# Three heads per softmax transpose and value matmul, spread by masked copies, in a two-layer recurrent-memory attention kernel

## The chip, the cores and the metric

The kernel runs on one core of one Trainium2 chip. The metric is device time in microseconds (us), from the first to the last instruction of one launch; the figure given for a kernel is the median of its runs. The engines are named as the profile names them: PE (TensorE matmuls), PEld (TensorE weight loads), DVE (VectorE), ACT (ScalarE), POOL (GpSimd) and SP (the queue from which most transfers are issued).

## What is computed

The reference runs two identical layers over 2048 tokens of width 512. A layer is attention with a recurrent memory (A), followed by a gated feed-forward part (B), each behind a layernorm and a residual. Cut to what matters:

```python
# A: 64 segments of 32 tokens; 8 memory rows go from one segment to the next
for s in range(64):
    h = concatenate([mem, x[s*32:(s+1)*32]])        # 40 rows of 512
    q, k, v = h @ Wq, h @ Wk, h @ Wv                # 32 heads of 128
    scores = where(mask, (q @ k.T) * 128**-0.5, -1e9)   # 40 x 40 per head
    o = softmax(scores) @ v                         # 40 x 128 per head
    o = sum over heads and features of o * Wo       # 40 x 512
    mem = o[:8];  out[s] = o[8:]
# B: (sigmoid(x @ w_gate) * (x @ w_up)) @ w_down, hidden width 1792
x = x + A(layernorm(x)); x = x + B(layernorm(x))    # twice
```

The memory makes a layer's attention a chain of 64 segments: segment s+1 can't form its queries before segment s has been multiplied by Wo.

## The kernel before

**Steps.** Both layers run at once, the second one six segments behind the first (`LAG`), so there are 70 steps (`emit_step`). In 58 of them two segments, one of each layer ("jobs"), share every instruction: their 2 x 40 = 80 columns stand side by side in the tile `hT` (512 features on 128 partitions x 4 chunks). In the first six and last six steps there is one job with 40 columns.

**One step** works through the 32 heads in six groups: five of six heads and one of two. A group is three "units", and a unit is a pair of heads (k, 16+k). For each group:

- Q and K (L730): per head 2 x 4 matmuls of 128x128 weights against 80 columns; one ACT copy per three heads takes them into `qku` (L1024; three such tiles).
- scores (L744): one matmul per head. The weights are the head's Q from `qku`, read as 80 columns; the moving operand is its K.
- softmax on DVE and ACT: mask added per job (L758), maximum, subtraction, exponential (L768), sum, reciprocal, product (L775) into `pb`, in which every head has 64 columns, 40 of them used.
- transpose (L787): one matmul per unit turns two heads of `pb` (80 rows x 128 columns) into 128 rows x 80 columns. The keys of the first head of the pair land on partitions 0 to 39, those of the second on 64 to 103.
- spread: two copies per group, on ACT (L1024) or DVE (L1026), take these two partition ranges into `ptsb`. Each head has its own column range there, and the rest of `ptsb` was zeroed once at the start, so that the tile is block-diagonal: in a head's columns only that head's rows are not zero.
- values (L808): one matmul per unit and job. The weights are 104 rows of `vsb` (the values of both heads, at the same partitions), the moving operand is 2 heads x 40 columns of `ptsb`.
- output (L826): after an ACT copy into `otsb`, 4 matmuls per head accumulate the product with Wo in one bank `WB`, from which DVE writes the next step's memory columns (L839).

**Values.** Most rows of V don't depend on the memory. They are computed in blocks ahead of time (`v_pass`, L584), written to DRAM (`scr`) and fetched per step (L685). The 16 rows of each job that touch the memory are computed in the step itself (`add_strips`, L698): 32 matmuls of 512 columns, two copies into the single tile `sst`, then eight transfers from `sst` to `vsb` (L710). `vsb` is three tiles of 1024 columns; a step uses two of them, one for heads 0 to 7 and 16 to 23, one for the others.

**The rest** is work of the feed-forward part (`ffn`: L926 gate and up, L950 down) and of `v_pass`; it fills PE between the steps' own work.

**Order.** Instructions are not issued in program order. `Planner` gets every piece of work as a task with an engine, a duration, what it reads and writes and which buffers it needs, and makes one fixed order per engine from them (`forward` and `backward`, 24 rounds, the one with the shortest planned span is kept). Engines then run that order strictly, each waiting for the others by semaphores. Durations are formulas in the code, such as these:

```python
def mm_ns(n):
    return max(n / 2.4 + 2.3, 26.0)
def copy_ns(n, half=False):
    return {"ACT": n * 0.833 + 52.0, "DVE": n / (1.92 if half else 0.96) + 73.0}
```

A task that names two engines (the spread copies do) is put on either by the planner. Copies that read one PSUM bank are not put on two engines at once.

## Time and profile before

| | before |
|---|---|
| median of 3 runs | 1829.39 us (1826.49 to 1831.26) |
| the profiled run, its time and its span | 1827.17 us, 1825.3 us |
| granted TensorE clock | 0.998 of full |
| ACT busy, DVE busy | 1194.2 us (65%), 1162.9 us (64%) |
| POOL busy | 569.9 us (31%) |
| transfers | 272.11 MB, mean 149 GB/s |
| scores L744: matmuls, columns | 1856 of 80 and 384 of 40 |
| transposes L787 | 1120 of 80 |
| value matmuls L808 | 2048 of 80 |
| spread copies | 546 on ACT, 294 on DVE |

How it is read: "busy" is the time in which at least one instruction of an engine was under way. The matmuls of one engine overlap: one takes about 200 ns from start to end, but the next one starts long before that. What a matmul costs is the time from its start to the start of the next one, and this is read from the timeline of a short window, where the profile merges like instructions into one row: start, time from first start to last end, engine, line, operation, tiles, shapes, and how many.

### The profile page before, as it was taken

To read this page: it belongs to the slowest core of one execution; us is meant where nothing else is said; L and a number is where in the kernel's file an instruction comes from. 1 tells how busy PE (TensorE), PEld (TensorE's weight loads), DVE (VectorE), ACT (ScalarE), POOL (GpSimd) and SP (SyncE) were. 2 spreads that over 40 slices of the span, in tenths; PEclk is the share of its full clock that TensorE was granted. 3 is DMA by queue.
4 is the path that set the end of the run, shared out by engine and by line. 5 is a ranking of instruction groups with operands and counts; after the bars stand their busy time and mean duration, and the time that the engine had idled before them with its cause. 6 is when DMAs were issued, how large, how long until landed. Compare 5 with 4: busy or idle time off the path is not lost.

```text
span 1825.3 us, 92117 instructions
## 1 busy us (share of the span) xinstructions
PE 1776.6 (97%) x39783; PEld 1533.6 (84%) x39970; DVE 1162.9 (64%) x3927; ACT 1194.2 (65%) x3005; POOL 569.9 (31%) x817
## 2 busy tenths in 40 slices
PE   7999999999999999999999999999999999999998
PEld 4678788988898888988898898888888898888886
DVE  5466655676666666666666667656666676656665
ACT  5666666676666666666666666666666666676664
POOL 5223032413233242413324141323324241333422
PEclk9999999999999999999999999999999999999999
DMA  9734254535445364535446363545536353544543
GB/s 351 233 108 148 62 155 121 163 100 176 147 153 157 103 204 122 170 109 169 149 124 187 109 194 100 170 131 155 158 110 196 117 168 95 173 144 127 174 124 107
DMA packets 138441, 272.11 MB, mean 149 GB/s; under 512 B 32954, under 2 KB 70594, under 8 KB 138034
## 3 DMA queue, kind: packets, MB, share of 16 engines
q0 software_dynamic: 56640, 183.09, 32.1%
q1 hardware_dynamic: 81394, 83.12, 15.4%
q8 instruction: 313, 5.13, 1.2%
q14 instruction: 94, 0.77, 0.1%
HBM read 221.85 MB, written 27.26 MB: 136 GB/s over the span
## 4 chain that ended last, share of the span: by engine, by line
PE 81%; DVE 9%; ACT 4%; SPq 3%; issue 2%; DMA 1%; POOLq 0%; ACTq 0%; DVEq 0%
PE bank L730 28%; PE bank L826 16%; PE bank L926 10%; PE bank L698 7%; PE bank L584 6%; PE bank L950 4%; PE bank L744 4%; PE bank L808 3%; DVE st L758 3%; SPq L485 3%; PE bank L787 2%; ACT ptsb L1024 1%; DVE pb L775 1%; DVE mx L763 1%; ACT qku L1024 1%
## 5 line engine op out<-in xcount | busy, mean ns | idle before, releaser
L730 PE MATMUL bank<-hT,wq_sb 128*128 128x80 bf16 (+1 forms) x8960 | 621.6, 198 | 3.5 <-issue 1.3
L730 PE MATMUL bank<-hT,wk_sb 128*128 128x80 bf16 (+1 forms) x8960 | 620.5, 198 | 3.2 <-DMA wk_sb<-in_A_Wk_dram 3.2
L1024 ACT CAST qku<-bank 128x480 bf16<-128x480 f32 (+3 forms) x770 | 391.1, 513 | 233.5 <-PE bank L730 165.7
L730 PEld LDWEIGHTS <-wq_sb 128*128 128x128 bf16 x8960 | 455.8, 99 | 38.5 <-issue 23.9
L730 PEld LDWEIGHTS <-wk_sb 128*128 128x128 bf16 x8960 | 450.6, 99 | 4.4 <-DMA wk_sb<-in_A_Wk_dram 3.6
L758 DVE TENSOR_TENSOR st<-bank,maskb 80x240 f32<-80x240 f32 (+1 forms) x732 | 267.9, 367 | 245.5 <-PE bank L744 238.7
L826 PE MATMUL bank<-otsb,wo_sb 128*128 128x80 bf16 (+1 forms) x8960 | 370.2, 198 | 9.6 <-ACT otsb L1024 8.1
L826 PEld LDWEIGHTS <-wo_sb 128*128 128x128 bf16 x8960 | 345.4, 99 | 35.0 <-issue 11.3
L918 POOL DMA_DIRECT2D wg<-in_B_w_gate_dram x217 | 164.7, 759 | 573.7 <-PE bank L926 520.2
L1024 ACT CAST otsb<-bank 128x480 bf16<-128x480 f32 (+3 forms) x420 | 199.9, 485 | 66.0 <-PE bank L808 51.7
L944 POOL DMA_DIRECT2D wd<-in_B_w_down_dram x217 | 154.2, 712 | 231.0 <-PE bank L744 88.7
L1024 ACT COPY ptsb<-bank 40x240 bf16<-40x240 bf16 (+3 forms) x546 | 170.8, 315 | 53.0 <-PE bank L787 46.0
L768 ACT ACTIVATE st<-st 80x240 f32<-80x240 f32 (+3 forms) x420 | 160.6, 383 | 45.8 <-DVE st L765 42.6
L770 DVE TENSOR_REDUCE mx<-st 80x6 f32<-80x240 f32 (+3 forms) x420 | 151.6, 364 | 50.7 <-ACT st L768 47.2
L926 PE MATMUL bank<-xnT,wg 128*128 128x128 bf16 (+2 forms) x1784 | 171.8, 218 | 2.0 <-issue 1.5
L926 PE MATMUL bank<-xnT,wu 128*128 128x128 bf16 (+2 forms) x1784 | 171.1, 218 | 0.0
L919 POOL DMA_DIRECT2D wu<-in_B_w_up_dram x217 | 162.7, 750 | 1.2 <-PE bank L926 0.5
L744 PE MATMUL bank<-qku 128*80 128x80 bf16 (+1 forms) x2240 | 160.2, 204 | 2.2 <-ACT qku L1024 1.6
L775 DVE TENSOR_TENSOR pb<-st,mx 80x240 bf16<-80x240 f32 (+3 forms) x420 | 154.9, 369 | 4.0
L765 DVE TENSOR_TENSOR st<-st,mx 80x240 f32<-80x240 f32 (+3 forms) x420 | 154.6, 368 | 4.2
L763 DVE TENSOR_REDUCE mx<-st 80x6 f32<-80x240 f32 (+3 forms) x420 | 153.0, 364 | 5.4
L543 POOL TENSOR_TENSOR lns<-lns,negh 128x1 f32<-128x1 f32 (+1 forms) x79 | 44.9, 570 | 357.0 <-DVE lns L542 319.7
(92 smaller groups left out, 2308.8 us busy)
## 6 DMA issues: line engine op xcount, KB each, us to landing
wg<-in_B_w_gate_dram POOLq DMA_DIRECT2D x220, 256.0 KB, 4.1
wu<-in_B_w_up_dram POOLq DMA_DIRECT2D x220, 256.0 KB, 4.5
wd<-in_B_w_down_dram POOLq DMA_DIRECT2D x220, 256.0 KB, 4.5
vsb<-scr SPq DMA_DIRECT2D x508, 48.0 KB
vsb<-sst SPq DMA_DIRECT2D x512, 32.0 KB
scr<-vst SPq DMA_DIRECT2D x136, 96.0 KB
wq_sb<-in_A_Wq_dram SPq DMA_DIRECT2D x10, 384.0 KB
wk_sb<-in_A_Wk_dram SPq DMA_DIRECT2D x10, 384.0 KB
```

The costliest lines, as they stand in the source:

```text
L730: nc.tensor.matmul(o_ap, lhsT=W[:, c, h * P:(h + 1) * P], rhs=mv(c), start=(c == 0), stop=(c == DC - 1))
L744: nc.tensor.matmul(s_all(SB)[full, w0 + i, :], lhsT=qku[:, i, 0, full], rhs=qku[:, i, 1, 0:ncol], start=True, stop=True)
L758: pl.add("DVE", dve_ns(n, True), lambda gsz=gsz, hs=hs, st=st, SB=SB, pj_=pj_, npj_=npj_, mk=mk, idx=idx: nc.vector.tensor_tensor(out=st[p ...
L763: pl.add("DVE", dve_ns(n), lambda hs=hs, st=st, mx=mx: nc.vector.tensor_reduce(out=mx[pr, hs], in_=st[pr, hs], axis=AX.X, op=ALU.max), r=s ...
L765: pl.add("DVE", dve_ns(n), lambda gsz=gsz, hs=hs, st=st, mx=mx: nc.vector.tensor_tensor(out=st[pr, hs], in0=st[pr, hs], in1=mx[pr, hs].uns ...
L768: pl.add("ACT", act_ns(n), lambda hs=hs, st=st: nc.scalar.activation(out=st[pr, hs], in_=st[pr, hs], func=ACTF.Exp, scale=self.scale), r=s ...
L775: nc.vector.tensor_tensor(out=pb[pr, hs, 0:L], in0=st[pr, hs], in1=rs[pr, 0:gsz].unsqueeze(2).to_broadcast([npart, gsz, L]), op=ALU.mult)
L826: nc.tensor.matmul(WB[:, c * ncol:(c + 1) * ncol], lhsT=self.wo[:, h, c * P:(c + 1) * P], rhs=otsb[:, hl, 0:ncol], start=(h == 0 and c == ...
L918: pl.add("POOL", 760, lambda wg=wg, fs=fs: nc.gpsimd.dma_start(out=wg[:], in_=self.wgv[:, :, fs]), r=[("wo", self.H - 1)], w=[gk] + bt, la ...
L919: pl.add("POOL", 760, lambda wu=wu, fs=fs: nc.gpsimd.dma_start(out=wu[:], in_=self.wuv[:, :, fs]), r=[("wo", self.H - 1)], w=[uk] + bt, la ...
L926: nc.tensor.matmul(gu[:, 2 * i + k, 0:n], lhsT=W[:, c, i * P:(i + 1) * P], rhs=xnT[:, c, rw], start=(c == 0), stop=(c == DC - 1))
L1024: nc.scalar.copy(out=dst, in_=src)
```

## The change

Units become triples: `NU` = 11 units, unit u holding heads u, u+11 and u+22 (the last unit has two). Groups are two units, still five groups of six heads and one of two.

- **Transpose.** `pb` holds heads at 40 columns instead of 64, so 128 consecutive columns hold three heads and the first eight columns of the next. One transpose per unit, and in single-job steps its moving operand has 40 columns instead of 80.
- **Spread.** All three heads' keys now stand on partitions 0 to 119. Three copies per group read all of them and multiply by a per-partition column of `rowm`, which is 1 on the rows of head i and 0 elsewhere. On ACT that is an activation `Copy` with the column as `scale`, on DVE a `tensor_scalar` multiplication. Zeroing `ptsb` beforehand is gone.
- **Values.** One matmul per unit and job with 120 rows of `vsb` against 3 x 40 columns.
- **Scores.** The weight operand is read as 128 columns instead of 80; `qku` is zeroed whole at the start so that what lies behind the 80 is defined.
- **Buffers.** `qku` 3 to 4 tiles; `sst` 1 to 2; `vsb` from three tiles of 1024 columns to two of 1408, each holding a whole step. The transfers to `vsb` per step of two jobs: six from `scr` (before: eight) and twelve from `sst` (before: eight), since `sst` pieces are cut at multiples of 8 and of 11 heads.
- **Start and end.** Weight loads come in pieces of two heads instead of three. The start's memsets go from DVE to POOL. `xo` is dropped: the last residual is written into `xa` and sent out from there; the initial memory is staged in a part of `hff`. Small constant tiles are packed together.

The diff, cut to what the prediction speaks of:

```diff
-        self.HH = H // 2
+        self.NU = (H + 2) // 3
+        self.units = [list(range(u, H, self.NU)) for u in range(self.NU)]
...
+        cuts = sorted(set(range(0, H + 1, 8)) | {min(i * self.NU, H) for i in range(4)})
+        self.pieces = [(a, b - a) for a, b in zip(cuts, cuts[1:])]
...
-        self.qku = [c.tile([P, 3, 2, LW], BF16, name=f"qku{i}") for i in range(3)]
-        self.vsb = [c.tile([P, 2, 1024], BF16, name=f"vsb{i}") for i in range(self.NV)]
+        self.qku = [c.tile([P, 3, 2, LW], BF16, name=f"qku{i}") for i in range(4)]
+        self.vsb = [c.tile([P, 2, self.NU * P], BF16, name=f"vsb{i}") for i in range(self.NV)]
...
-        self.sst = [c.tile([P, 2, 512], BF16, name=f"sst{i}") for i in range(1)]
+        self.sst = [c.tile([P, 2, 512], BF16, name=f"sst{i}") for i in range(2)]
...
-            pl.add("DVE", 320, lambda t_=t_: nc.vector.memset(t_[:], 0.0), w=[("qkz", k)])
+            pl.add("POOL", 500, lambda t_=t_: nc.gpsimd.memset(t_[:], 0.0), w=[("qkz", k)])
...
-                        nc.tensor.matmul(s_all(SB)[full, w0 + i, :], lhsT=qku[:, i, 0, full], rhs=qku[:, i, 1, 0:ncol],
+                        nc.tensor.matmul(s_all(SB)[:, w0 + i, :], lhsT=fview(qku[:, i, 0, 0:1], [(1, P)]), rhs=qku[:, i, 1, 0:ncol],
...
-                    nc.tensor.transpose(out=pt[:, ul * LW:(ul + 1) * LW], in_=pb[full, 2 * ul:2 * ul + 2, :].rearrange("p i k -> p (i k)"),
-                                        identity=self.ident[full, full])
...
-                pl.add(("ACT", "DVE"), copy_ns(nu * nj * L, True), spread, r=[PB], w=[("ptsb", pi, i)])
+                    nc.tensor.transpose(out=pt[:, ul * ncol:(ul + 1) * ncol], in_=pb[pr, 3 * L * ul:3 * L * ul + P],
+                                        identity=self.ident[pr, pr])
...
+            for i in range(min(3, gsz)):
+                def spread(i=i, nu=nu, ptsb=ptsb, PB=PB, nr=nr):
+                    pt = PB[0:nr, 0:nu * ncol // 2].bitcast(BF16).rearrange("p (u j q) -> p u j q", u=nu, j=nj)
+                    return (fview(ptsb[0:nr, 0, i, 0:1], [(nj * 3 * L, nu), (3 * L, nj), (1, L)]), pt, self.rowm[0:nr, i:i + 1], None)
+
+                pl.add(("ACT", "DVE"), copy_ns(nu * ncol, True), spread, r=[PB], w=[("ptsb", pi, i)])
...
-                                         lhsT=self.vsb[halves[u // 8]][0:64 + L, j, (u % 8) * P:(u % 8 + 1) * P],
-                                         rhs=ptsb[0:64 + L, ul * nj + idx, :, :], start=True, stop=True)
+                        nc.tensor.matmul(fview(OB[:, o:o + 1], [(ncol, nh), (1, L)]),
+                                         lhsT=self.vsb[vh][0:nh * L, j, u * P:(u + 1) * P],
+                                         rhs=ptsb[0:nh * L, ul * nj + idx, 0:nh, :], start=True, stop=True)
...
+                    if tk.on == "ACT":
+                        nc.scalar.activation(out=got[0], in_=got[1], func=ACTF.Copy, scale=got[2])
+                    else:
+                        nc.vector.tensor_scalar(out=got[0], in0=got[1], scalar1=got[2], scalar2=None, op0=ALU.mult)
```

## The prediction

> **What bounds the kernel now.** I read the page's busy table and chain first, then a window of steady steps, then the groups by form, then a short timeline.
>
> ```profile
> PE 1776.6 (97%) x39783; PEld 1533.6 (84%) x39970; DVE 1162.9 (64%) x3927; ACT 1194.2 (65%) x3005; POOL 569.9 (31%) x817
> PE 81%; DVE 9%; ACT 4%; SPq 3%; issue 2%; DMA 1%; POOLq 0%; ACTq 0%; DVEq 0%
> ```
>
> PE is busy 97% of the span and makes up 81% of the chain that ended last. A busy PE need not be a fast one, so its pace has to be checked.
>
> ```profile
> 800.00:1000.00 200.00, 197.35 (x4429) 174.56 (x4445) 126.84 (x423) 130.15 (x320) 65.67 (x91) 1.00 0.50 150
> 922.00:924.00 2.00, 2.00 (x61) 2.00 (x58) 2.00 (x7) 1.63 (x5) 0.00 (x0) 1.00 0.13 33
> 924.00:926.00 2.00, 2.00 (x55) 1.99 (x52) 1.92 (x7) 2.00 (x7) 0.00 (x0) 1.00 0.00 0
> ```
>
> Columns: window, its length, busy time of PE, PEld, DVE, ACT, POOL, then clock and DMA share. Over 200 us PE is idle for 2.65 us only. But inside a step, where the softmax runs, DVE and ACT are nearly full too: from 922 to 932 they are busy 9.42 and 8.24 of 10 us. That is where a rival can come from.
>
> The pace of PE, in the timeline (start, time, ..., count; the next row's start less this one's, over the count, is the cost of one):
>
> ```profile
> 922.06 0.40 PE L744 MATMUL bank<-qku 128*80 128x80 bf16 x6
> 922.29 0.28 PE L787 MATMUL bank<-ident,pb 80*128 80x80 bf16 x3
> 922.41 0.31 PE L730 MATMUL bank<-hT,wq_sb 128*128 128x80 bf16 x4
> 922.55 0.31 PE L730 MATMUL bank<-hT,wk_sb 128*128 128x80 bf16 x4
> ...
> 923.95 0.38 PE L808 MATMUL bank<-ptsb,vsb 104*128 104x80 bf16 x6
> 924.17 0.40 PE L744 MATMUL bank<-qku 128*80 128x80 bf16 x6
> 924.39 0.39 PE L553 MATMUL bank<-ident,xn 128*128 128x128 bf16 x4
> 924.62 0.38 PE L808 MATMUL bank<-ptsb,vsb 104*128 104x80 bf16 x6
> ...
> 1795.55 0.25 PE L730 MATMUL bank<-hT,wk_sb 128*128 128x40 bf16 x4
> 1795.65 0.39 PE L744 MATMUL bank<-qku 128*80 128x40 bf16 x6
> 1795.88 0.26 PE L730 MATMUL bank<-hT,wq_sb 128*128 128x40 bf16 x4
> ```
>
> So 80 columns cost 36 ns at L730 (0.143/4 over a longer run of rows), 37 at L808, 38 at L744 and 40 at L787 in threes; 128 columns cost 57 (L553, 0.23/4); 40 columns cost 25 at L730 (0.10/4), but a score of 40 columns still costs 38 (0.23/6). The cost is nearly proportional to columns: PE is working at its own rate, and work taken from it should shorten the span.
>
> ```profile
> L744 PEld LDWEIGHTS <-qku 128*80 128x80 bf16 x2240 | 126.2, 121 | 18.5 <-ACT sst L1024 5.5 <-ACT qku L1024 2.6 <-issue 1.7
> L730 PEld LDWEIGHTS <-wq_sb 128*128 128x128 bf16 x8960 | 455.8, 99 | 38.5 <-issue 23.9
> ```
>
> Loading 80 columns of score weights takes longer (121 ns) than loading 128 (99).
>
> **What the Trainium skill says.** "TensorE: Matmul & The Clock Gate", section Back-to-back issue gap, gives N/2.4 + 2.5 ns for a matmul of N columns and a floor near 25 ns; the trace agrees (36, 57, 25). The same page, section Weight-path perf modes, says that the fast weight load needs a weight of exactly 128 columns; the two rows above agree. "ScalarE: Activation LUTs", section What ACT_TABLE_LOAD costs, says that a per-partition pointer operand adds about 93 ns to an ACTIVATE and that back-to-back ones overlap by about 93; no run here shows the first, and of the second below.
>
> **The change, part by part.** Counts of after are those of the built program.
>
> *Transposes.* 1120 become 638 of 80 columns and 132 of 40. At 37.5 ns (between 36.7 in sixes and 40 in threes) 42.0 us become 23.9 + 132 x 26 = 27.4: **-14.6 us**.
>
> *Values.* 2048 of 80 columns become 1280 of 120 and 128 of 80, the same 163,840 columns. 120 columns cost 36 + 40 x 20/48 = 53 ns (between 80 and 128): 2048 x 36.7 = 75.2 us become 67.8 + 4.7 = 72.5: **-2.7 us**. Two thirds as many matmuls save only the fixed part.
>
> *Scores.* With 128 weight columns 1856 go from 38.3 to 36 ns and 384 from 38 to 25: 4.3 + 5.0 = **-9.3 us**.
>
> All three lie on PE with work queued behind them, so they count in full: -26.6 us. Lower end: 36 ns for every transpose and 2 ns for scores of 80 columns, -24. Upper end: PE also loses time at each switch between kinds of work; from the starts of all matmuls, waits within, a transpose occupies 44.6 ns, a value matmul 45.4, a score 46. If this extra goes with the instructions, the sum is about -40.
>
> *Spread.* 840 copies become 1190 (816 on ACT, 374 on DVE), of 160 elements instead of 240 for a six-head group: the elements stay, a third fixed part comes. Today's pair on ACT and a pair of another kind in the same bank:
>
> ```profile
> 922.78 0.73 ACT L1024 COPY ptsb<-bank 40x240 bf16<-40x240 bf16 x2
> 934.11 0.43 ACT L1024 CAST oxT<-bank 128x128 bf16<-128x128 f32 x2 [0.81 <-PE bank L826]
> ```
>
> The pair does not overlap: 0.364 us each, of which 240 x 0.83 = 200 ns are elements and 164 fixed. The oxT pair does overlap (0.27 each alone, 0.16 apart). Three copies at 160 x 0.83 = 133 ns of elements take 3 x 190 + 107 = 677 ns if they overlap like oxT, 3 x 297 = 891 if not, and 3 x 390 = 1170 if the page's 93 ns come on top. I take 800 against 730 today: the new copies start on one partition like oxT, but carry a pointer. On DVE, 0.57 us for a pair becomes three of about 243 (160 fixed, 83 of elements), 729; up to 981 if the multiplication ran at one element per cycle.
>
> This sits on each group's path from transpose to values. From all 420 groups' starts in the trace, the value matmul follows the last transpose by 1.39 us in the median, 1.04 in the lower quartile, 0.9 at a tenth; its floor on ACT is 0.235 + 0.73 + 0.05 = 1.01. So about a fifth already stand at the floor, and above it a quarter lies within 0.35 us. A path longer by g then costs PE about 0.2 g + g x g/2800 (ns) per group: 16 ns for g = 70. ACT spreads 3.4 groups a step (68% of five), in some 64 steps' worth: 3.4 us, taken as **+3** (lower end 0).
>
> *Buffers.* The second `sst` removes ACT's wait before its strip copies (18.7 us for the DMA that last read `sst`), of which PE saw 5.5 us, in the row above; I take **-3**, 0 and -5.5 being the ends. A fourth `qku`: PE waits 1.6 us for `qku` in all; 0. `vsb`: a tile comes free a whole step ahead, and PE waits 0.2 us for it today; 0. SP issues 18 transfers a step for `vsb` instead of 16; behind the strips stand the other transfers of the step. At 0.67 us apart (eight strips from 937.87 take 5.37 us) twelve take 8 us, but first values follow the strips by 11 us (937.14 to 948.14) and the first group's pieces go first; 0, hidden behind Q and K.
>
> *Start.* Packets of wq and wk shrink from 768 to 512 bytes. In the first 70 us, 256 bytes take 18 ns and 768 take 38, so 512 about 28: 7.9 MB take 27 us of the 16 DMA engines instead of 24. PE waits 3.2 us for wk today; **+1** of 0 to 3. POOL gets 15 memsets. By its rows now (128 elements 0.20 us, 40 elements 0.13) those put ahead of the first layernorm's power take 3.7 us after three new setup operations of some 0.5, ending near 6.1 us; the power starts at 6.63. Cost 0, at most 2; DVE loses 3.2 us of memsets ahead of its first statistics, which could start them a little sooner, counted 0.
>
> *End.* The last residual goes into another tile by the same instruction and transfer; 0.
>
> Sum: -26.6 + 3 - 3 + 1 = -25.6 on a span of 1825.3, the profiled run's. The profiled run took 1827.17, the median is 1829.39; the same difference gives **1804 us**. This is 1.4% less.
>
> **The rivals.**
>
> A, *more than counted*: the switching extra goes with the instructions, and waits for `sst` vanish: -40 - 5.5 + 2 gives 1786. For: the 44 to 46 ns per slot above. Against: much of it is waiting that remains. Chance 0.13.
>
> B, *hidden anyway*: what PE saves comes back as waits within the step, because the softmax of a step is paced by DVE and ACT, full from 922 to 932. Saved 0.38 us a step, given back for the most part: 1826. Against: PE waits 8.1 us for `otsb` and 4.1 for `ptsb` in all. Chance 0.13.
>
> C, *slower, ACT takes over*: a masked copy costs 390 ns start to start, neither overlapped nor free of the pointer's price. Path +440 ns: 0.2 x 440 + 440 x 440/2800 = 157 ns per group on ACT, 34 us over 3.4 x 64 groups. ACT gains 1.5 us a step where it has 1.8 left in ten; its queue holds the exponentials and `otsb`, whose waits (12.2 us with `ptsb`) I double. 1829 - 27 + 34 + 12 = 1848. It decides from about 370 ns per copy. For: the pair that doesn't overlap. Against: that pair starts on partitions 0 and 64, the new ones don't. Chance 0.14.
>
> That the change does not do what it says is excluded by the built counts.
>
> **How the numbers follow.** Forecast (1795 to 1815) 0.60, A 0.13, B 0.13, C 0.14. No change is within 0.3%, 1823.9 to 1834.9. Faster: 0.60 + 0.13 and half of B, 0.79; the same 0.08; slower 0.13. The range goes from 1781 (most of A) to 1831 (most of B).
>
> **What would show it.** Right: L787 x770 and L808 x1408; scores' weight loads near 99 ns and 36 ns apart; PE still 96% or more; `ptsb` copies under 300 ns apart; PE's wait for `ptsb` under 10 us. Wrong: `ptsb` copies at 370 ns or more, waits of PE for `ptsb` and `otsb` of tens of us, or a first matmul of queries well after 28.5 us.

## The result: 0.4% slower, and the profile after

| | before | after |
|---|---|---|
| median, range | 1829.24 us (1826.49 to 1831.26) | 1836.66 us (1835.23 to 1840.07) |
| ratio to before | | 1.0044, 95% interval 1.0025 to 1.0064 |
| profiled run: span, clock | 1825.3 us, 0.998 | 1834.2 us, 0.994 |
| PE time if every matmul ran at its pace (see below) | 1726.8 us | 1711.5 us |
| the rest of the span: waits and half clock | 98.5 us | 122.7 us |

The forecast was 1804 us, 1.4% less. Measured were 7.4 us more than before, and 32.7 more than forecast. The last two rows say in short what happened. They are worked out, not read: for every matmul in the built order of PE the pace of the timeline is taken, N/2.4 + 2.3 ns for N columns and not under 25 ns, which gives 36 ns for 80 columns and 52 for 120; 57.5 ns stand for one of the strips' 512-column matmuls, of which four run side by side. The sum is taken from the span. By this count PE does have 15.3 us less to do. But it loses 24.2 us more in between, so that the saving came back as waiting, and some more. (The slow score loads, which the prediction put at 9.3 us, stand in the second of these rows, before only; without them the loss grew by yet more.)

The page of the changed kernel, busy times and chain:

```profile
PE 1782.3 (97%) x38980; PEld 1517.2 (83%) x38980; DVE 1176.2 (64%) x4025; ACT 1226.4 (67%) x3237; POOL 573.2 (31%) x835
PE 78%; SPq 8%; DMA 6%; ACT 5%; DVE 2%; issue 1%; ACTq 0%; DVEq 0%
```

PE's busy time hides the loss: 97% as before. The chain shows it: the SP queue and the DMAs hold 14% of it, before it was 4%. The waits of PE name the place (columns: engine, line, what it waited for, us in total, times, the longest):

```profile
PE bank L819 <- DMA vsb<-sst: 14.4, 25, 1.7
PE bank L533 <- DMA hff<-in_A_mem_dram: 5.4, 1, 5.4
PE bank L740 <- DMA wk_sb<-in_A_Wk_dram: 5.2, 5, 1.6
PE bank L838 <- ACT otsb L1040: 3.4, 15, 0.5
...
PE bank L819 <- ACT ptsb L1032: 2.1, 4, 0.9
```

The value matmuls (L819) now wait for the transfers of the strips (`vsb<-sst`); in the kernel before, the only wait of a value matmul for a transfer that this view listed was 0.2 us. PE's waits for `otsb` and `ptsb`, on which the forecast watched for a slower ACT, fell instead, to 3.4 and 2.1 us. In the kernel before they were 8.1 and 4.1:

```profile
PE bank L826 <- ACT otsb L1024: 8.1, 30, 0.6
PE bank L808 <- ACT ptsb L1024: 4.1, 15, 0.6
```

Where along the span the time goes is a second question. The first Q of a step in one trace less the same in the other says how far the changed kernel is behind: 2.6 us at step 0, 7.2 at step 1, 13.1 at step 6, 10.7 at step 7, 7.0 at step 60, 10.4 at step 69, and 8.9 at the end. So all of the 8.9 us between the spans are already there when the steps with two jobs begin; after that the saving and the new waits roughly cancel. Up to 60 us the 16 DMA engines are full in both kernels, and after the change they move less (the last two columns are their share and GB/s; before, then after):

```profile
30.00:60.00 30.00, 27.48 (x280) 15.63 (x283) 12.31 (x36) 17.60 (x36) 13.01 (x25) 0.94 1.07 368
30.00:60.00 30.00, 26.83 (x317) 14.98 (x315) 13.01 (x40) 17.31 (x36) 13.93 (x26) 1.00 1.09 351
```

One step shows how the wait for strips comes about. The timeline from 1018 us, SP's queue, strips and their copies:

```profile
1024.57 1.91 PE L705 MATMUL bank<-wv_sb,hT 128*32 128x512 bf16 x32
1025.66 0.59 ACT L1040 CAST sst<-bank 128x512 bf16<-128x512 f32 x1 [0.57 <-PE bank L705]
...
1026.53 0.59 ACT L1040 CAST sst<-bank 128x512 bf16<-128x512 f32 x1 [0.28 <-PE bank L705]
...
1027.29 3.46 SPq L719 DMA_DIRECT2D vsb<-sst  x4
1030.80 0.54 SPq L692 DMA_DIRECT2D vsb<-scr  x1
1031.38 6.23 SPq L719 DMA_DIRECT2D vsb<-sst  x8
```

and PE in the same step:

```profile
1035.26 0.87 PE L819 MATMUL bank<-ptsb,vsb 120*128 120x120 bf16 x5 [0.52 <-ACT th L943]
1037.73 0.48 PE L819 MATMUL bank<-ptsb,vsb 120*128 120x120 bf16 x3 [1.60 <-DMA vsb<-sst]
...
1038.14 0.63 PE L938 MATMUL bank<-xnT,wg 128*128 128x128 bf16 x4
```

The planner put the strips (L705) 6.6 us after the step's first Q. Two of the twelve transfers hold SP for 1.58 and 1.88 us, the others for 0.5 to 0.6; what held these two is not shown. The eighth is issued at 1034.50 and has landed at 1037.68, and only then can the value matmuls of the second group go on, after 1.6 us of standing. (The first group of a step needs the first six transfers, the second the first eight. In the kernel before, both needed only the first four of eight.) Four gate matmuls of 128 columns then take 0.42 us from start to start (1038.14 to 1038.56) where they take 0.23 at full rate: the clock is at half.

### The profile page after: what moved, and what is told of

It is laid out like the page before. It is cut to its first block, busy times and chain, and to the rows that moved or that the text cites. A ratio compares the mean times of both kernels' runs of the same rounds, so it can differ in the third digit from the quotient of the medians.

```text
span 1834.2 us, 90612 instructions
## 1 busy us (share of the span) xinstructions
PE 1782.3 (97%) x38980; PEld 1517.2 (83%) x38980; DVE 1176.2 (64%) x4025; ACT 1226.4 (67%) x3237; POOL 573.2 (31%) x835
## 4 chain that ended last, share of the span: by engine, by line
PE 78%; SPq 8%; DMA 6%; ACT 5%; DVE 2%; issue 1%; ACTq 0%; DVEq 0%
PE bank L740 26%; PE bank L838 15%; PE bank L938 9%; PE bank L705 7%; PE bank L591 7%; SPq L719 5%; PE bank L962 5%; DMA vsb<-sst 4%; PE bank L819 4%; PE bank L754 3%; SPq L490 2%; ACT ptsb L1032 2%; PE bank L797 1%; ACT otsb L1040 1%; DMA wk_sb<-in_A_Wk_dram 1%
## 5 line engine op out<-in xcount | busy, mean ns | idle before, releaser
L768 DVE TENSOR_TENSOR st<-bank,cst 40x240 f32<-40x240 f32 (+3 forms) x768 | 278.6, 367 | 201.9 <-PE bank L754 194.5
L838 PE MATMUL bank<-otsb,wo_sb 128*128 128x80 bf16 (+1 forms) x8960 | 366.0, 198 | 5.0 <-ACT otsb L1040 3.4
L1032 ACT ACTIVATE ptsb<-bank,cst 120x160 bf16<-120x160 bf16 (+3 forms) x816 | 253.3, 383 | 29.7 <-PE bank L797 23.1
L1040 ACT CAST otsb<-bank 128x480 bf16<-128x480 f32 (+3 forms) x420 | 204.0, 493 | 63.3 <-PE bank L819 49.3
L780 DVE TENSOR_REDUCE small<-st 80x6 f32<-80x240 f32 (+3 forms) x420 | 151.3, 362 | 56.3 <-ACT st L778 53.9
L819 PE MATMUL bank<-ptsb,vsb 120*128 120x120 bf16 (+1 forms) x1408 | 142.4, 215 | 20.4 <-DMA vsb<-sst 14.4
L754 PE MATMUL bank<-qku 128*128 128x80 bf16 (+1 forms) x2240 | 155.9, 198 | 1.2 <-issue 1.1
L775 DVE TENSOR_TENSOR st<-st,small 80x240 f32<-80x240 f32 (+3 forms) x420 | 154.6, 369 | 3.7
L550 POOL TENSOR_TENSOR small<-small,cst 128x1 f32<-128x1 f32 (+1 forms) x79 | 44.1, 560 | 358.3 <-DVE small L549 342.7
L785 DVE TENSOR_TENSOR pb<-st,small 80x240 bf16<-80x240 f32 (+3 forms) x420 | 153.1, 368 | 3.4
```

Source lines behind the costliest of these rows:

```text
L754: nc.tensor.matmul(s_all(SB)[:, w0 + i, :], lhsT=fview(qku[:, i, 0, 0:1], [(1, P)]), rhs=qku[:, i, 1, 0:ncol], start=True, stop=True)
L768: pl.add("DVE", dve_ns(n, True), lambda gsz=gsz, hs=hs, st=st, SB=SB, pj_=pj_, npj_=npj_, mk=mk, idx=idx: nc.vector.tensor_tensor(out=st[p ...
L775: pl.add("DVE", dve_ns(n), lambda gsz=gsz, hs=hs, st=st, mx=mx: nc.vector.tensor_tensor(out=st[pr, hs], in0=st[pr, hs], in1=mx[pr, hs].uns ...
L819: nc.tensor.matmul(fview(OB[:, o:o + 1], [(ncol, nh), (1, L)]), lhsT=self.vsb[vh][0:nh * L, j, u * P:(u + 1) * P], rhs=ptsb[0:nh * L, ul * ...
L838: nc.tensor.matmul(WB[:, c * ncol:(c + 1) * ncol], lhsT=self.wo[:, h, c * P:(c + 1) * P], rhs=otsb[:, hl, 0:ncol], start=(h == 0 and c == ...
L1032: nc.scalar.activation(out=got[0], in_=got[1], func=ACTF.Copy, scale=got[2])
```

## The experiments

Kernels named "own order" keep each engine's order as the planner made it for the changed kernel (or for the one before), so that only the edit differs. All ratios are to the kernel before on the same chip. Where two kernels of different occasions are compared, their ratios are subtracted and the difference taken of 1829 us; the changed kernel's ratio is 1.0044.

**Are the strips' transfers hidden?** Leave them out, after the first filling of each value tile, in both kernels, each in its own order. The values are then computed with old strips.

```diff
-  pl.add("SP", 430, lambda ...: nc.sync.dma_start(out=self.vsb[vh][...], in_=fview(sb[...])))
+  skip = t - j * LAG >= 2 and name == "vs"
+  pl.add("SP", 430, lambda ..., skip=skip: None if skip else nc.sync.dma_start(...))
```

(in the kernel before, which has three value tiles, from 3 on)

> The changed kernel in its own order on every engine, with the transfers from sst to vsb left out after each vsb tile has been filled once (so the memory rows of V are stale; every matmul and copy stays). Theory 'strips': in the changed kernel PE waits about 20 us for these twelve transfers a step and loses 3.4 us of clock after such waits; without them the time falls by 15 to 25 us to 1812 to 1822. Rival 'ACT' (the masked copies hold PE up): the waits move to ptsb and otsb, and the time falls by 5 us at most.

> The same leaving-out in the kernel before, in its own order: transfers from sst to vsb only until each tile has been filled once. Its trace shows PE waiting 0.2 us for vsb. Theory 'strips': the eight transfers a step are hidden, the time moves by less than 4 us (1825 to 1831). Rival 'these transfers always cost, by DMA traffic or by the SP queue': it falls by 10 us or more, as in the changed kernel.

| | median (range) | ratio [95%] |
|---|---|---|
| changed kernel, no strip transfers | 1816.12 us (1814.51 to 1816.58) | 0.9934 [0.9922, 0.9947] |
| kernel before, no strip transfers | 1825.34 us (1823.25 to 1829.61) | 0.9989 [0.9982, 0.9995] |

So the transfers cost the changed kernel 20 us (1.0044 less 0.9934) and the kernel before 2. The list of waits has 14.4 us for the value matmuls and 19.2 for the loads of their weights:

```profile
PEld L819 <- DMA vsb<-sst: 19.2, 29, 1.8
```

The forecast's 0 is refuted, for the changed kernel alone. The mechanism is read from the two orders: counting PE's work, at the pace above, that stands between the last strip matmul and the first value matmul of a step (steps 8 to 59), the median is 12.0 us before and 8.7 after, the least 7.7 and 7.2. Against this stand the transfers: from the first one's issue until the last has left SP, the eight of a step took 5.8 us in the median before, and the twelve take 8.8. The window above, with 10.3, is one of the longest.

**Do the masked copies cost more than their own path?** Make them plain ones, own order; the masking is left out, so each head's columns also hold the other heads' weights. Then both edits together.

```diff
-  nc.scalar.activation(out=got[0], in_=got[1], func=ACTF.Copy, scale=got[2])
+  nc.scalar.copy(out=got[0], in_=got[1])
...
-  nc.vector.tensor_scalar(out=got[0], in0=got[1], scalar1=got[2], scalar2=None, op0=ALU.mult)
+  nc.vector.tensor_copy(out=got[0], in_=got[1])
```

> The changed kernel in its own order, with the three spread copies of a group as plain copies, without the multiplication by rowm (so a head's columns also hold the other heads' rows: the masking is left out). An ACT copy should end some 100 ns sooner than the 402 ns of the masked one. Theory 'strips, start and narrow weights': PE waits 5.5 us for ptsb and otsb in all, so the time falls by at most 5 us, 1831 to 1837. Rival C of the prediction 'ACT takes over': three times 0.1 us per group off a saturated path brings 10 us or more.

> The changed kernel in its own order, with both the strip transfers after the first fill of each value tile left out and the three masked copies made plain ones (so old strips and unmasked weights enter the values). If the two losses sit in different places (the strips ahead of the first value matmuls of a step, the copies at every group), they add: 1836.7 - 20.5 - 16.8 = 1799 us, 1796 to 1804, which is where the forecast of 1804 stood without them. If both loosen the same slack of ScalarE and PE, most of the second gain is already in the first: 1808 to 1815 us.

| | median (range) | ratio [95%] |
|---|---|---|
| changed kernel, plain copies | 1819.81 us (1813.46 to 1822.08) | 0.9951 [0.9937, 0.9965] |
| changed kernel, plain copies and no strip transfers | 1794.13 us (1793.18 to 1797.10) | 0.9815 [0.9803, 0.9828] |

Plain copies are worth 17 us alone (1.0044 less 0.9951) and 22 us where the strips are gone (0.9934 less 0.9815). The expectation that the sum of PE's waits for `ptsb` and `otsb`, 5.5 us, would bound it was wrong. The two losses add: 42 us together, and the 5 us by which this exceeds 20 and 17 are within the four intervals. The groups by shape (columns: busy us, mean ns of one, then idle before) show what a mask costs. The changed kernel:

```profile
L1032 ACT ACTIVATE ptsb<-bank,cst 120x160 bf16<-120x160 bf16 x609 | 199.1, 402 | 17.4 <-PE bank L797 13.6 <-DVE ptsb L1034 2.0 <-DVE small L782 0.2
L1034 DVE TENSOR_SCALAR ptsb<-bank,cst 120x160 bf16<-120x160 bf16 x261 | 65.1, 290 | 13.4 <-ACT ptsb L1032 8.7 <-PE bank L797 3.3
```

and with plain copies:

```profile
L1032 ACT COPY ptsb<-bank 120x160 bf16<-120x160 bf16 x609 | 141.6, 309 | 21.7 <-PE bank L797 18.5 <-DVE ptsb L1034 0.7
L1034 DVE COPY ptsb<-bank 120x160 bf16<-120x160 bf16 x261 | 49.4, 229 | 14.4 <-ACT ptsb L1032 7.5 <-PE bank L797 6.0
```

402 against 309 ns on ACT, 290 against 229 on DVE: the masked form costs 93 and 61 ns more. Three such copies in a row on ACT take 965 ns in the median from the first start to the last end, three plain ones 684, and the pair of the kernel before 718. So plain copies undo the masks' price and some 35 ns besides. The loss does not appear as a large wait anywhere: with plain copies PE's wait for `ptsb` goes from 2.1 to 1.0 us, for `otsb` from 3.4 to 3.0, and that for the strips even rises from 14.4 to 17.6. As far as the records of the two traces can be compared (some matmuls are missing in one), it lies for the most part in the switches from one kind of matmul to the next. In the four kinds of switch that fell most, time beyond the pace from the last transpose to a value matmul behind it falls from 6.2 to 2.5 us, from scores to output matmuls from 3.8 to 0.9, from values to output from 6.4 to 4.3, from scores to values from 3.7 to 1.9, about 10 us of the 13.8 us that separate the two spans. It comes off evenly: the start of step 6 is 0.5 us earlier with plain copies, of step 40 9.2, of step 60 13.3.

In the chain of the kernel without both losses, PE is nearly all that is left:

```profile
PE 91%; SPq 3%; DVE 2%; ACT 2%; issue 1%; DMA 1%; ACTq 0%; DVEq 0%
```

**Parts alone.** The scores' 128-column weights in the kernel before (own order); 80-row transposes in the single-job steps of the changed kernel (own order); the first Q and K weights in equal pieces (own order); the two strip buffers laid on one tile (own order); and the buffers added to the first of these (planned anew, since the planner counts buffers).

```diff
kernel before, score weights of 128 columns
-  lhsT=qku[:, i, 0, full]
+  lhsT=fview(qku[:, i, 0, 0:1], [(1, P)])
changed kernel, 80-row transposes
-  in_=pb[pr, 3 * L * ul:3 * L * ul + P], identity=self.ident[pr, pr]
+  in_=pb[full, 3 * L * ul:3 * L * ul + P], identity=self.ident[full, full]
changed kernel, one tile for both strip buffers
-  self.sst = [c.tile([P, 2, 512], ...) for i in range(2)]
+  self.sst = [c.tile([P, 2, 512], ...) for i in range(1)] * 2
changed kernel, heads of the weight pieces: 2, 3, 3, 3 in place of 2, 2, 2, 2, 2, 1
kernel before, score weights as above and: sst 1 -> 2, qku 3 -> 4, vsb 3 -> 2
```

> The kernel before in its own order, only with the score weights read as 128 columns instead of 80 (the further output rows are not read). The prediction's step: scores cost 36 instead of 38 ns at 80 columns and 25 instead of 38 at 40, 9.3 us less: 1818 to 1822. Rival 'the slower weight load was hidden behind other waits': 1825 to 1829.

> The changed kernel in its own order, but in the twelve single-job steps the transposes use all 80 rows of pb and 80 columns, as before the change, instead of 40 rows and 40 columns. Theory 'narrow weights': the matmul after a transpose of 40 rows starts 109 ns after it instead of 36, and two such transposes are 39 apart; 69 times 73 ns less plus 63 times 2 gives 5 us, and part of the clock loss at the start may go with it: 1828 to 1833. Rival 'columns count, rows don't': 132 transposes of 80 columns cost 10 ns more each, so it is 1 us slower, 1837 to 1839.

> The changed kernel in its own order, with wq and wk loaded in pieces of 2, 3, 3 and 3 heads (768-byte packets, 24 transfers) instead of 2, 2, 2, 2, 2 and 1 (512-byte packets, 34 transfers). Theory 'start': the last piece of wk lands some 3 us earlier, so the second step starts 3 to 4 us earlier: 1832 to 1834. Rival 'the start is held by the layernorms and memsets on POOL': no change, 1836 to 1838.

> The changed kernel in its own order, with both strip buffers laid on one tile, so that a copy of strips has to wait for the transfers out of the one before. The prediction's step (second buffer worth 3 us) gives 1839 to 1841 us. If the copies come so late after the transfers of the step before that one buffer is free anyway, 1835 to 1838. If a copy at the head of ScalarE's queue now waits for transfers that are themselves late, 1845 or more.

> The kernel before with the score weights read as 128 columns, and with the buffers of the change: two strip buffers, four Q/K tiles, two value tiles. If the buffers bring the 3 us that the prediction gave them, 1818 to 1819.5 us (the score weights alone gave 1821.7). If they bring nothing, 1821 to 1823; if two value tiles in place of three bind the strips, 1825 or more.

| | median (range) | ratio [95%] | against |
|---|---|---|---|
| before, score weights of 128 | 1821.73 us (1820.72 to 1824.57) | 0.9977 [0.9967, 0.9987] | -4.2 us to before |
| changed, 80-row transposes | 1833.31 us (1832.55 to 1840.34) | 1.0037 [1.0024, 1.0049] | -1.3 us to changed |
| changed, equal weight pieces | 1837.40 us (1834.77 to 1846.26) | 1.0060 [1.0043, 1.0077] | +2.9 us to changed |
| changed, one strip tile | 1844.18 us (1839.66 to 1846.23) | 1.0086 [1.0073, 1.0099] | +7.7 us to changed |
| before, score weights and buffers | 1831.95 us (1828.90 to 1835.91) | 1.0023 [1.0017, 1.0030] | +8.4 us to the first row |

The first row is the smallest part of the change in code, and alone it makes the kernel before faster, by 4.2 us from the ratios and 5.9 between the spans. The load takes 99 ns for 121:

```profile
L744 PEld LDWEIGHTS <-qku 128*128 128x128 bf16 x2240 | 109.5, 99 | 19.7 <-ACT sst L1024 5.5 <-ACT qku L1024 2.6 <-issue 1.3
```

The transposes explain a small loss at both ends of the changed kernel. Its timeline in a single-job step:

```profile
1808.64 0.21 PE L797 MATMUL bank<-cst,pb 40*128 40x40 bf16 x2
1808.79 0.24 PE L754 MATMUL bank<-qku 128*128 128x40 bf16 x3
```

and the same place with 80 rows:

```profile
1805.42 0.24 PE L797 MATMUL bank<-cst,pb 80*128 80x80 bf16 x2
1805.50 0.23 PE L754 MATMUL bank<-qku 128*128 128x40 bf16 x3
```

Two transposes of 40 rows hold PE for 150 ns, two of 80 rows, with twice the columns, for 80. Over all of the trace a 40-row transpose takes 39 ns up to another one and 109 up to anything else, which happens 69 times: 63 x 39 + 69 x 109 ns = 10.0 us, where the forecast took 132 x 26 = 3.4. At 35 ns each they would take 4.6. Against the changed kernel the run shows a gain of that order at most: the spans differ by 2.2 us, and the two ratios' intervals overlap.

Equal weight pieces shorten step 0 by 3.0 us, but that kernel's trace has 34.1 us at half clock where the changed kernel's has 20.5, which by the estimate of half the work lost costs it 6.8 us elsewhere, so nothing is left. Whether the smaller pieces cost anything is not settled by this run. (Below, in another order, both edits together, 80-row transposes and equal pieces, do gain.)

With one strip tile the kernel is 7.7 us slower by the ratios. The traces differ by 3.8 us only, since the profiled run is the fastest of its five; 4.9 us arise in steps 6 and 7: step 6 is the one in which two sets of strips are computed, and ACT there waits for the first set's transfers:

```profile
ACT sst L1040 <- DMA vsb<-sst: 6.1, 2, 4.1
```

Two waits in all. In the steady steps one tile would do. The last row does not isolate the buffers: a step of the kernel before uses two of the three value tiles, so that leaving it two takes away the lead of a step, which the changed kernel, with whole-step tiles, keeps. Its 8 us say nothing on the other buffers.

**Does the loss belong to the change, or to the order planned for it?** The planner takes SP to be busy for 430 ns with each strip transfer; in the traces they are issued 0.63 us apart in the median and 0.73 to 0.74 in the mean, before as after. It takes a masked copy to be as long as a plain one. First the price of the strips alone, planned anew; then the same with 80-row transposes and equal pieces, which change no price, so that the order is that of the first; then with the copies' price besides, planned anew.

```diff
strip price
-  pl.add("SP", 430, lambda i4=i4, ...
+  pl.add("SP", 640, lambda i4=i4, ...
copy price
-  pl.add(("ACT", "DVE"), copy_ns(nu * ncol, True), spread, ...
+  pl.add(("ACT", "DVE"), {e: v + {"ACT": 95.0, "DVE": 60.0}[e] for e, v in copy_ns(nu * ncol, True).items()}, spread, ...
```

> The changed kernel, with the planner's price for issuing one transfer from sst raised from 430 to 640 ns, which is nearer to what the trace shows (0.6 to 0.67 us apart); nothing else is changed, but the order is planned anew. In the new order the median of PE's work between the end of the strips and the first value matmul is 11.4 us, in the changed kernel's order 8.7, in the order before 12.0. Theory 'strips': most of the 14 us of waits for vsb go, 1817 to 1827. Rival 'the transfers are too many wherever they stand': 1832 to 1840.

> The changed kernel with the dearer strip transfers in the plan, transposes of all 80 rows in the single-job steps, and weight pieces of three heads. If the three effects add up (12 to 16, 3 and 0 to 3 us): 1812 to 1821, faster than both kernels. If the new order only moves the waits: above 1827.

> The changed kernel, its order planned with what the trace shows: a masked copy 95 ns dearer on ScalarE and 60 ns dearer on VectorE, a strip transfer 640 ns, 80-row transposes in the single-job steps and the first Q/K weights in equal pieces. If the losses come from an order planned with prices that are too low, this ends under the version without the copies' price (1826.7): 1815 to 1822 us. If ScalarE and VectorE have no free place for the longer copies wherever they are put, 1825 to 1829 us.

A new price also draws a wholly new order, so luck has to be measured. A "draw" below changes one price that has nothing to do with the change by 1 ns:

```diff
-    WAIT = 65.0
+    WAIT = 66.0      (or 64.0)
```

> The changed kernel with its order planned anew, one unrelated price (the planner's charge for a second wait) 66 ns in place of 65. If the draw of an order matters little, 1833 to 1840 us like the changed kernel. If the changed kernel's own order is an unlucky draw, 1815 to 1828.

> The same with 64 ns. Little effect of a draw: 1833 to 1840 us. An unlucky draw before: 1815 to 1828. With the run at 66, the distance of the three orders is a first measure of what a draw moves.

> The changed kernel with the planner's price of a masked copy alone corrected (95 ns dearer on ScalarE, 60 ns on VectorE); strips still 430 ns. If the wrong price of the copies costs what the all-prices version won by it (14 us), 1820 to 1825 us. If that was the draw, it lies where the two draws lie, about 1836.

> The version planned with all measured prices (1812.9 us), its order drawn again with 66 ns in place of 65 for the unrelated price. If the right prices are the cause of its time, 1809 to 1818 us. If it was a lucky draw, 1820 to 1830.

> The kernel before with its order planned anew, the unrelated price 64 ns in place of 65. If a new draw costs the kernel before as much as the changed one, 1840 us or more. If its order is robust because its first values stand some 12 us after the strips wherever the planner puts them, 1824 to 1833 us.

> The changed kernel with the strip price, the 80-row transposes and the equal pieces, but the copies still at the price of plain ones, drawn again with 66 ns. If the copies' price is needed, 1822 to 1830 us as in the first draw (1826.7). If it is not, and 1826.7 was an unlucky draw, 1807 to 1815 us.

| order planned with | first order | another draw |
|---|---|---|
| before: its own prices | 1829.24 us; 1 | 1830.06 us (1829.18 to 1833.60); 1.0018 [1.0008, 1.0028] |
| changed: its own prices | 1836.66 us; 1.0044 | 66: 1835.67 us (1824.97 to 1839.59); 1.0034 [1.0011, 1.0057] |
| | | 64: 1861.68 us (1859.77 to 1867.30); 1.0192 [1.0173, 1.0210] |
| changed: copy price only | 1851.74 us (1842.68 to 1857.33); 1.0127 [1.0096, 1.0159] | |
| changed: strip price only | 1831.28 us (1830.77 to 1834.96); 1.0029 [1.0017, 1.0040] | |
| changed: strip price, 80 rows, equal pieces | 1826.70 us (1822.39 to 1830.19); 0.9994 [0.9986, 1.0002] | 1830.80 us (1824.86 to 1832.25); 1.0016 [1.0009, 1.0023] |
| changed: all of these and the copy price | 1812.86 us (1806.27 to 1818.99); 0.9913 [0.9894, 0.9931] | 1807.79 us (1807.46 to 1810.18); 0.9896 [0.9880, 0.9913] |

This follows. The one draw of the kernel before moved it by 3 us, the two of the changed kernel by -2 and +27, of which the last lies outside both expectations. All three orders of the changed kernel wait for strips, 14.4, 17.7 and 20.8 us of PE in the list; the work between strips and first values is 8.4 to 8.7 us in the median in all three. One price alone brings little: with the strips' price their waits fall to 0.8 us, but the time stays at 1831 us where 1817 to 1827 were expected; with the copies' price it grows to 1852, above both expectations, and the strips' waits are the most of these runs (31.9 us of PE). In the order with the strips' price, 80 rows and equal pieces are worth 6 us by the ratios (1.0029 less 0.9994, intervals apart), which still is not the 1812 to 1821 expected. And with both prices right the two draws lie at 1808 and 1813 us, below every order with one of them wrong, by 0.8% and more (0.9994 less 0.9913), and faster than both kernels. The 80-row transposes and the equal pieces are in them too, but with these and without the copies' price the two orders are as slow as the kernel before. The kernel before was not planned anew with a right price for its strips, so how much that would bring there is not known. PE's waits of the second order at both prices:

```profile
PE bank L825 <- DMA vsb<-sst: 6.2, 11, 1.4
...
PE bank L844 <- ACT otsb L1046: 3.2, 10, 0.8
PE bank L825 <- ACT ptsb L1038: 2.8, 10, 0.5
```

Without the copies' price (first draw) they are

```profile
PE bank L844 <- ACT otsb L1046: 7.5, 28, 0.6
PE bank L825 <- ACT ptsb L1038: 7.4, 25, 0.7
```

There the strips are all but gone from the list (0.5 us), and the waits for `otsb` and `ptsb` stand in their place; with the copies' price in the plan they fall from 14.9 us to 6.0. The work of PE between strips and first values is 11.3 us in the median in the order at 1808 us, and never under 8.3, against 8.7 and 7.2 in the changed kernel's.

The slowest draw shows how a pause of PE grows. SP and PE, from two answers of its timeline:

```profile
421.06 5.65 SPq L719 DMA_DIRECT2D vsb<-sst  x8
```

```profile
428.33 0.23 PE L819 MATMUL bank<-ptsb,vsb 120*128 120x120 bf16 x1 [1.80 <-DMA vsb<-sst]
428.39 2.36 PE L838 MATMUL bank<-otsb,wo_sb 128*128 128x80 bf16 x35
```

and three stretches around it (columns: window, length, busy PE, PEld, DVE, ACT, POOL, clock, DMA share, GB/s):

```profile
424.00:428.00 4.00, 2.36 (x37) 1.80 (x33) 3.25 (x14) 4.00 (x15) 3.01 (x4) 1.00 0.61 153
428.60:432.00 3.40, 3.40 (x53) 3.40 (x50) 1.19 (x6) 0.56 (x1) 0.00 (x0) 0.50 0.54 164
434.00:438.00 4.00, 3.95 (x95) 3.74 (x93) 0.33 (x2) 2.16 (x7) 1.30 (x3) 1.00 0.79 229
```

After a pause of 1.8 us the granted clock is 0.50 for 3.41 us: 53 matmuls start in 3.4 us where 95 start in 4 later. This order has 47.8 us at half clock in all, of which six such stretches lie between 425 and 1790 us close behind waits for strips; the changed kernel has 20.5 us and the kernel before 6.8. If half of it is lost, these are 23.9, 10.2 and 3.4 us. So by this estimate 13.7 of the 31.4 us between the spans of this draw and of the changed kernel are clock.

## Why the prediction was wrong

**What failed.** Three terms of the sum. The first two account for more than the whole miss of 32.7 us, the third adds to it, and a larger gain than forecast in the later steps took part of it back.

*Strips for `vsb`, "0, hidden behind Q and K".* Measured 20 us, against 2 in the kernel before. The length of the twelve transfers, put at 8 us, was nearly right (8.8 in the median). What failed is the cover. "First values follow the strips by 11 us" was read from the kernel before and carried over to the new one; there the planner leaves 8.7 us of work in the median, 7.2 at the least (before, counted likewise, 12.0 and 7.7). That the first group's pieces go first was right, but they are six transfers now and were four. The order is not a property that the change keeps: it is planned again, and at 430 ns for a transfer the planner gives the twelve 5.2 us. The built order could have been counted before the run, like the instructions were.

*Spread, "+3".* Measured +17, or +22 once the strips are out of the way. The Trainium skill, "ScalarE: Activation LUTs", section What ACT_TABLE_LOAD costs, has the 93 ns for a pointer operand, and the trace agrees exactly (402 less 309). What was mis-sized is the length of a group's copies. In the step of the result, on ACT,

```profile
1038.70 0.69 ACT L1032 ACTIVATE ptsb<-bank,cst 120x160 bf16<-120x160 bf16 x2
```

two masked copies take 0.69 us where one takes 0.40, so they start 0.29 apart. Over the trace three take 965 ns in the median, for the 800 taken; the pair before takes 718, for 730. So a group's copies on ACT grew by 247 ns and not by 70. (Three plain ones take 684, where the prediction had 677: it was right on how the copies overlap and took too little for the mask.) Put into the prediction's own formula, 0.2 g + g x g/2800, 247 ns give 71 ns per group and 15.5 us in all, close to the 17 measured. That is agreement in size only: the formula speaks of value matmuls that wait for `ptsb`, and this wait fell to 2.1 us. The runs show a loss spread over many switches instead. ACT has to do most of the copies, and those of Q and K, the exponentials and `otsb` stand behind them in one queue; that this is how the loss spreads is argued, not shown. That the planner didn't know of the length made it worse: planned with the right prices, the same copies cost far less (the last row of the table of orders). The rival of a slower ACT named this engine, but its price (390 ns start to start, where 277 are the median) and its sign (waits for `ptsb` and `otsb` of tens of us, which didn't come) don't describe what happened.

*Start, "+1 of 0 to 3".* Measured 7.2 us at step 1 and 13.1 at step 6. Every traced kernel with the change, whatever its order, begins step 1 between 2.8 and 9.2 us later than the kernel before, and step 6 between 6.0 and 17.7 (other orders and versions of the kernel before with its three value tiles: -0.1 to 2.4, and -0.6 to 2.0). The packets were priced well: 512 bytes take 28 ns, as forecast. But only PE's own wait for wk was charged with them, and the six steps with one job were not looked at as a stretch of their own. In the one trace with equal pieces step 0 is shorter by 3.0 us of the 4.6 by which it grew; half of the slow 40-row transposes and 10.2 us at half clock between 125 and 147 us (3.4 before) lie in these steps too. What each is worth, and what the rest is, stays open.

**What was off in size.**

- Scores: -9.3 forecast, -4.2 measured alone (5.9 between the spans). The pace itself was right, 36 ns for 80 columns and 25 for 40; where the rest went is not shown.
- Transposes in single-job steps: 3.4 us forecast, 10.0 by pace and count. A weight that fills fewer rows was priced by its columns; the rows were not asked about.
- Second strip buffer: -3 forecast for "ACT's wait", and the wait of PE's weight loads behind `sst` that it should remove rose from 5.5 to 10.2 us. Its worth is 7.7 us by the ratios; as far as the one trace shows, it lies in the one step with two sets of strips, where 4.9 us arise. (The 18.7 us on which the term rested stand in the view under `vsb<-scr`, a transfer that doesn't read `sst`.)
- Rival A's "about -40": the prediction's own figures give less. 350 transposes fewer at 7.1 ns over the pace and 640 value matmuls fewer at 8.7 add 8.1 us to 26.6, about -35.

**What held.** Without the first two of these terms, the sum of the forecast was -26.6 - 3 + 1 = -28.6 us. The changed kernel without strips and masks, against the kernel before without strips, gives 0.9989 - 0.9815, or 31.8 us less. But this agreement is in part luck. By the traces that version is 10.1 us behind the kernel before at step 6, where the forecast has +1, and 34.1 ahead at the end, so that it gains 44 us over the later steps, where the forecast has 26.6 + 3. The larger gain and the later start cancel. The runs don't divide the gain further; leaving the masks out also shortens the three copies below what the change could have, and that more of the switches' time went with the instructions, as rival A has it, is not excluded. 120 columns were put at 53 ns and take 52. That PE's own rate bounds the kernel, once those two losses are out, was right: the chain of that version has PE at 91%.

**The rivals.** "Hidden anyway" (1826 us) came nearest in time, by another mechanism: softmax on DVE and ACT was to pace the step, and it was the strips on SP. That a transfer would become the wait was dismissed in one sentence where it should have been a rival with a price: twelve transfers at 0.67 to 0.8 us are 8 to 10 us, against 7.7 us of cover at the least and 12.0 in the median in the order of the kernel before.

## What to carry to other kernels

Where a planner makes the order, a change is two changes, the work and the order; count in the newly built order how much work covers each transfer that you call hidden, and compare it with the transfers' measured spacing and with how many of them the first user needs, before you write 0. Update the planner's prices with the change: here the changed kernel took 1836 to 1862 us with the old prices, and 1808 to 1813 with the measured ones (and two small edits, worth 6 us in another order). Price a new form of an instruction as often as it runs in a row: 93 ns more on a copy became 247 on a group. Its loss need not show as one wait. And compare the starts of the steps, not only the spans: here the whole difference was there by the seventh step.

## What the runs showed that I had not expected

- A transpose whose weights fill 40 rows holds up whatever follows: 109 ns (69 places) where one with 80 rows takes 35 to 42. The Trainium skill, "TensorE: Matmul & The Clock Gate", section Step-by-step: what each phase is for, says that the rows of a weight don't matter to the time of its load; for the load the trace agrees (95 ns for 40 rows, 100 for 80). The 109 ns are beyond that statement, and their cause is not shown.
- Some pauses of PE cost twice. The same page, section What's actually happening, has the clock drop to half after an idle window of about 3.4 us that runs freely. The stretches at 0.50 in the traces are 3.41 us long or whole multiples of it, which agrees; but pauses of 1 to 2 us were enough. Of those over 1.2 us after the first 30 us, 3 of 5 in the changed kernel have such a stretch with them, and 6 of 13 in the one with the copies' price only, where one of 2.03 us at 1124 us has none. Some stretches follow shorter pauses only: before the one at 125.9 us in the changed kernel the longest is 0.58 us. At half rate a stretch loses about 1.7 us of work, half of 3.41.
- Moving one unrelated price of the planner by 1 ns moved the changed kernel by 27 us (ratio 1.0192 for 1.0044), the kernel before by 3.
- Two masked copies that start on the same partition overlap in part (two take 0.69 us, one 0.40), where in the kernel before a pair that starts on different partitions took 0.73 us at 0.35 each. The two kinds differ in shape too, so that the partition is the cause is not shown.
